# Seven tokens per row, early weight casts, and reciprocals over the GpSimd queue in a fused attention and maxout kernel

## The chip, the cores and the metric

One core of one Trainium2 chip. The time is device microseconds of one execution, as the median over several runs. In the profiles, PE is the matmul engine, PEld its weight loads, DVE the vector engine, ACT the activation engine, POOL GpSimd, and SP the engine that only issues DMAs (SPq is its instruction queue). A run is called slow if it took over 1.5% more than the fastest run of the same kernel; comparisons use the other ("fast") runs.

## The reference

```python
# q, k, v: 8 batches x 12 heads x 448 tokens x 64, float32
scores = cap * tanh(q @ k.T / sqrt(64) / cap)        # cap = 30
attn   = exp(scores - max);  attn /= attn.sum(-1)
x      = (attn @ v)  as (8*448 tokens) x 768
g      = maximum(x @ w1, x @ w2)                     # 768 -> 1024
out    = g @ w_out                                   # 1024 -> 768, float32
```

The kernel computes the last part as relu(x @ (w1 - w2)) @ w_out + x @ (w2 @ w_out); `wd` is the difference, `wm` the product.

## The kernel before

Work goes pair by pair of heads: 48 pairs (numbered 0 to 47), six to a batch. Three pairs share one load of q, k and v (a group), and three share one set of reciprocals of the softmax sums. While a pair's scores go through ACT, PE is filled with matmuls of the batch before. A batch has 448 = 3 x 128 + 64 tokens, so the tokens of a batch stand as three full tiles and a half one, and the two halves of two batches share a tile (`t == 3` below). An SBUF partition p holds the tokens 3p, 3p+1, 3p+2 of the first 384.

Parts (cuts marked):

```python
def invert(g, n0=0, n1=G):            # reciprocals of one group's sums
    nc.vector.reciprocal(t[:m, :], sums[g, n0][:m, :])
    nc.sync.dma_start(out=d[:m, :], in_=t[:m, :])           # "write": SBUF -> DRAM, rec_d
    for h in range(2):                                      # "spread": DRAM -> 64 partitions, rec_b
        nc.sync.dma_start(out=rb[64*h : 64*h+64, ...], in_=flat[h:h+1, :, :].to_broadcast(...))

def moe(b):                            # one batch of the second part
    ...                                # x @ wd -> relu -> g ; then, per tile t of 128 tokens:
        if t == 3:
            ...                        # 64 rows each to two batches
        else:
            rows = out[b0*S : b0*S + NJ*P, :].rearrange("(p j) n -> p j n", j=NJ)
            nc.sync.dma_start(out=rows[:, j, :], in_=osb)   # one DMA of 128 rows of 3072 B

for i in range(N):                     # pair i
    pv_main(i); ...; gather(g)         # sums of a group: SBUF -> SBUF by DMA, after its third pair
    F(8); qk(i+1, 3); ex(i+1, 4, 7)    # F(n): n matmuls of the fill
    for f, a in todo[i]: f(*a)         # this pair's loads and GpSimd casts
    F(6); transposes(i+2); F(6)
    if i >= G and n == 0: invert(g - 1)      # first pair of a group: the group before
    if i >= G and n == 1: normalize(g - 1)   # xT = u * rec_b on GpSimd
    qk(i+2, 0); qk(i+2, 1); ...
```

## Time and profile before

Median 392.37 us of 3 runs (392.2 to 392.74); the profiled execution has a span of 390.3 us at a mean clock of 0.983.

I cut the span in three by the first tanh of pair 11 and of pair 44, as the timeline has them: the start (transfers and ACT bound it, and the weights are prepared), the middle (PE bounds it) and the tail.

| before | us |
|---|---|
| start, to the first tanh of pair 11 | 86.7 |
| middle, pairs 11 to 44 | 225.2 |
| tail, to the end of the span | 78.4 |

The lines of the profile itself stand in the prediction.

### The profile page before, as it was taken

The page shows a single profiled execution, that of the slowest core. Times are in us where ns is not written, and L with a number is a line of the kernel's source. Part 1 is how long each engine was busy: PE and PEld are TensorE (multiplying, and loading weights), DVE is VectorE, ACT ScalarE, POOL GpSimd, SP SyncE. Part 2 cuts the span into 40 slices and gives each one's busy share as a digit, 9 for nine tenths or more (in the row PEclk, how much of TensorE's full clock was granted, in tenths as well). Part 3 has the DMA queues.
Part 4 walks back from the last instruction along what each step waited for, and adds up shares of the span by engine and source line. Part 5 has one row for each costly group of instructions (what it writes and reads, how often), then busy time and mean ns, then how long its engine had stood idle before and what let it go on. Part 6 is the DMA issues. An engine that isn't in the chain of part 4 may idle for free.

```text
span 390.3 us, 5720 instructions
## 1 busy us (share of the span) xinstructions
PE 358.5 (92%) x2128; PEld 171.8 (44%) x2128; DVE 164.3 (42%) x248; ACT 292.4 (75%) x289; POOL 199.6 (51%) x254
## 2 busy tenths in 40 slices
PE   3468896999999999989998999999999999999995
PEld 1123443544444444434443445444444444455563
DVE  5332657774434533253325433352345333633421
ACT  2699995878899799978998899889998899400000
POOL 4272269674638374656657464729482733651000
PEclk9995998999999999999999999999999999999999
DMA  6998899786779768967989597969796751322022
GB/s 142 280 252 180 242 288 274 198 202 165 149 199 252 198 171 199 260 181 192 217 225 223 142 237 210 255 166 225 219 188 179 166 142 65 90 73 100 23 81 81
DMA packets 106596, 71.50 MB, mean 183 GB/s; under 512 B 61384, under 2 KB 99400, under 8 KB 106568
## 3 DMA queue, kind: packets, MB, share of 16 engines
q1 hardware_dynamic: 104616, 67.99, 67.6%
q0 software_dynamic: 1952, 3.15, 4.6%
q8 instruction: 16, 0.26, 0.3%
q14 instruction: 12, 0.10, 0.1%
HBM read 53.48 MB, written 11.18 MB: 166 GB/s over the span
## 4 chain that ended last, share of the span: by engine, by line
PE 54%; DMA 17%; ACT 7%; SPq 6%; POOL 6%; DVE 5%; issue 3%; POOLq 0%; DVEq 0%; ACTq 0%
PE mm L318 15%; PE mm L333 11%; PE mm L330 9%; PE pv L250 8%; DMA rec_d<-rec_s 7%; DMA rec_b<-rec_d 6%; POOL xT L305 6%; PE s L231 5%; ACT expo L238 3%; ACT tanh L232 3%; DMA vm<-in_v_dram 3%; PE pv L259 2%; SPq L112 2%; SPq L101 1%; DMA xT<-in_moe_w_dram 1%
## 5 line engine op out<-in xcount | busy, mean ns | idle before, releaser
L232 ACT ACTIVATE tanh<-s 128x896 bf16<-128x896 f32 x144 | 126.0, 909 | 36.2 <-PE s L231 35.9
L305 POOL TENSOR_TENSOR xT<-u,rec_b 64x448 bf16<-64x448 f32 x95 | 108.2, 1139 | 86.1 <-DMA rec_b<-rec_d 73.8
L238 ACT ACTIVATE expo<-tanh 128x1792 bf16<-128x1792 bf16 x96 | 144.9, 1510 | 3.0
L265 DVE COPY u<-pv 128x896 f32<-128x896 f32 x48 | 52.3, 1091 | 105.3 <-PE pv L259 80.6
L333 PE MATMUL mm<-wo_sb,gT 128*128 128x384 bf16 x448 | 88.8, 327 | 0.0
L318 PE MATMUL mm<-xT,wd_sb 128*128 128x448 bf16 x384 | 80.8, 353 | 3.3 <-POOL xT L305 1.7
L330 PE MATMUL mm<-wm_sb,xT 128*128 128x384 bf16 x336 | 68.0, 327 | 1.8 <-DVE osb L337 1.8
L250 PE MATMUL pv<-expo,vp 128*128 128x448 bf16 x288 | 66.3, 367 | 1.1 <-ACT expo L238 1.1
L333 PEld LDWEIGHTS <-gT 128*128 128x128 bf16 x448 | 41.9, 98 | 36.5 <-issue 10.8
L337 DVE COPY osb<-mm 128x384 f32<-128x384 f32 x56 | 31.0, 555 | 59.9 <-PE mm L333 54.9
L318 PEld LDWEIGHTS <-wd_sb 128*128 128x128 bf16 x384 | 35.4, 98 | 43.9 <-issue 14.5
L231 PE MATMUL s<-qkT 64*128 64x448 bf16 x288 | 46.0, 370 | 7.7 <-DVE qkT L210 5.2
L322 DVE TENSOR_SCALAR gT<-mm 128x448 bf16<-128x448 f32 x64 | 39.9, 623 | 29.6 <-PE mm L318 28.6
L330 PEld LDWEIGHTS <-xT 128*128 128x128 bf16 x336 | 31.7, 98 | 28.6 <-issue 8.7
L250 PEld LDWEIGHTS <-vp 128*128 128x128 bf16 x288 | 28.2, 101 | 29.1 <-issue 7.7
L132 POOL CAST kqf<-qm 128x1152 bf16<-128x1152 f32 x15 | 17.2, 1147 | 33.9 <-DMA qm<-in_q_dram 33.7
L235 ACT ACTIVATE tanh<-s 128x448 bf16<-128x448 f32 x48 | 26.0, 542 | 4.3 <-PE s L234 4.1
L124 POOL CAST vp<-vm 128x576 bf16<-128x576 f32 x30 | 19.9, 665 | 14.2 <-DMA vm<-in_v_dram 9.4
L132 POOL CAST kqf<-km 128x1152 bf16<-128x1152 f32 x15 | 17.2, 1147 | 12.7 <-DMA km<-in_k_dram 11.9
L231 PEld LDWEIGHTS <-qkT 64*128 64x128 bf16 x288 | 10.9, 96 | 22.8 <-issue 15.1
L209 PE MATMUL mm<-ident,kqf 128*128 128x128 bf16 x96 | 9.8, 248 | 11.5 <-DVE kqf L132 7.7
L186 PE MATMUL mm<-wo_sb,w2T 128*128 128x384 bf16 x96 | 18.7, 328 | 0.0
(44 smaller groups left out, 158.9 us busy)
## 6 DMA issues: line engine op xcount, KB each, us to landing
rec_b<-rec_d SPq DMA_DIRECT2D x30, 336.0 KB, 5.0
out_dram<-osb SPq DMA_DIRECT2D x24, 384.0 KB, 3.9
km<-in_k_dram SPq DMA_DIRECT2D x15, 576.0 KB, 7.0
qm<-in_q_dram SPq DMA_DIRECT2D x15, 576.0 KB, 4.5
vm<-in_v_dram SPq DMA_DIRECT2D x15, 576.0 KB, 4.4
xT<-in_moe_w_dram SPq DMA_DIRECT2D x6, 512.0 KB
wo_sb<-in_moe_w_out_dram POOLq DMA_DIRECT2D x4, 384.0 KB, 7.3
gT<-in_moe_w_dram POOLq DMA_DIRECT2D x6, 256.0 KB, 5.8
```

The lines of the kernel that those rows point to most:

```text
L132: eng.tensor_copy(t[:, n0:n1, o : o + NJ, :].rearrange("p n j (h d) -> p n h j d", h=2), m[:, 2 * n0 : 2 * n1, :].rearrange("p (n h) (j d) ...
L231: nc.tensor.matmul(s[:, h, :S], t[r, j * P : (j + 1) * P], qTn[r, :])
L232: nc.scalar.activation(tanh[i][:, 2 * j : 2 * j + 2, :], s[:, :, :S], AF.Tanh, scale=scale / cap)
L238: nc.scalar.activation(expo[i][:, c0:c1, :], tanh[i][:, c0:c1, :], AF.Exp, scale=float(cap))
L250: nc.tensor.matmul(ps[:, h, :S], vp[g % 2][:, n, h, j, :], e[:, 2 * j + h, :], start=(j == 0), stop=False)
L265: nc.vector.tensor_copy(U[g][:, :, n, :], pvt[i][:, :, :S])
L305: eng.tensor_mul(xT[b // 2][r, hp, cs], U[g][r, h, n, :], rec[g, n0][r, n - n0, :])
L318: nc.tensor.matmul(ps[:, :S], wd_sb[:, c, f * P : (f + 1) * P], x[:, c, cs], start=(c == 0), stop=(c == KC - 1))
L322: nc.vector.tensor_relu(g[:, f, cs], ps[:, :S])
L330: nc.tensor.matmul(ps[:, : DM // 2], x[:, c, ts], wm_sb[:, c, hs], start=(c == 0), stop=False)
L333: nc.tensor.matmul(ps[:, : DM // 2], g[:, f, ts], wo_sb[:, f, hs], start=False, stop=(f == FC - 1))
L337: nc.vector.tensor_copy(osb[:, hs], ps[:, : DM // 2])
```

## The change

The intent: in the first two batches (groups 0 to 3, `NT = 4`) a partition row holds seven consecutive tokens, which makes the q and k loads one long row each, with no separate remainder; w_out and w2 are cast by DMA early; the reciprocals stand earlier in the order of work, and their write and spread leave SP for GpSimd's queue. The core of the diff, with cuts:

```diff
+    R7 = S // 64                          # 7
 def load(g, what, ...):
+        if g < NT:                        # q, k: one DMA, rows of 7 tokens
+            nc.sync.dma_start(out=t[...], in_=rows(src, b, h0, h1).rearrange(...))
 ...
 def transposes(i):
-        for j in range(8):                # 8 of 128x128
-            nc.tensor.transpose(ps[:, j*P:(j+1)*P], kqf[g%2][:, n, j, :], ident)
+        for c, to in todo:                # 13 blocks of 64 columns, two 64x64 each, and one 128x128
+            for a in range(2):
+                r = slice(64*a, 64*a+64)
+                nc.tensor.transpose(ps[r, to:to+64], x[r, c:c+D], ident[r, r])
 ...
+    def chain(g):
+        return nc.gpsimd if g > 0 else nc.sync
 def invert(...):
-        nc.sync.dma_start(out=d[:m, :], in_=t[:m, :])
+        chain(g).dma_start(out=d[:m, :], in_=t[:m, :])
+    def spread(...):                      # now a step of its own, on chain(g)
 ...
 def moe(b):
-                rows = out[b0*S : b0*S + NJ*P, :].rearrange("(p j) n -> p j n", j=NJ)
-                nc.sync.dma_start(out=rows[:, j, :], in_=osb)
+                j = t if t < 3 else t - 4
+                o = out[b*S : (b+1)*S, :]
+                if wide: ...              # batches 2 to 7: as before
+                else:
+                    o = o.rearrange("(r j) n -> j r n", j=R7)
+                    nc.sync.dma_start(out=o[2*j : 2*j+2, :, :], in_=osb)
 ...
+    for f in range(0, FC, 2): load_wo(f)  # before the loop, on GpSimd
+    for c in range(3):        load_w2(c)
 ... in the loop over pairs:
+        if i >= G and n == 0: invert(g - 1)         # after F(8) now
         qk(i+1, 3); ex(i+1, 4, 7); for f, a in todo[i]: f(*a)
+        if i >= G and n == 0: spread(g - 1)
+        elif i >= G and n == 1: normalize(g - 1)
         F(6); transposes(i+2); F(6)
-        if i >= G and n == 0: invert(g - 1)
-        if i >= G and n == 1: normalize(g - 1)
```

More of the change, by code (lines that the diff above doesn't have):

```diff
@@ L40 @@
     NJ = 3
+    NT = 4
+    R7 = S // 64
     scale = 1.0 / (D ** 0.5)
@@ L69, with flat @@
     qf = [t[:, :, 4:8, :] for t in kqf]
+    def flat(g):
+        return kqf[g % 2].rearrange("p n j c -> p n (j c)")
     ident = const.tile([P, P], bf16, name="ident")
@@ L89, in half, with rows, raw_of @@
         return slice(0, 64) if b % 2 == 0 else slice(64, P)
+    def rows(t, b, h0, h1):
+        return t[b, h0:h1, :, :].rearrange("h (r j) d -> (h r) (j d)", j=R7)
+    def raw_of(g, what):
+        if (g, what) not in raw:
+            raw[g, what] = stage.tile([P, 2 * L * NJ * D + (2 * L if what == "q" else L) * D], f32, name=what + "r")
+        t = raw[g, what]
+        m = t[:, : 2 * L * NJ * D].rearrange("p (h c) -> p h c", c=NJ * D)
+        l = t[:, 2 * L * NJ * D :].rearrange("p (h d) -> p h d", d=D)
+        return t, m, l
     def load(g, what, n0=0, n1=L):
@@ L94, in load @@
         src = {"k": k, "q": q, "v": v}[what]
-        if (g, what) not in raw:
-            raw[g, what] = (
-                stage.tile([P, 2 * L, NJ * D], f32, name=what + "m"),
-                stage.tile([P, 2 * L if what == "q" else L, D], f32, name=what + "l"),
+        t, m, l = raw_of(g, what)
+        if g < NT and what == "v":
+            x = rows(src, b, h0, h1).rearrange("(h r) c -> r h c", r=64)
+            for a in range(2):
+                nc.sync.dma_start(
+                    out=m[64 * a : 64 * a + 64, 2 * n0 : 2 * n1, :], in_=x[:, :, NJ * D * a : NJ * D * (a + 1)]
+                )
+            for par in range(2):
+                nc.sync.dma_start(
+                    out=l[64 * par : 64 * par + 64, n0:n1, :], in_=x[:, par::2, 2 * NJ * D :]
+                )
+            return
+        if g < NT:
+            nc.sync.dma_start(
+                out=t[:, n0 * S : n1 * S].rearrange("p (n c) -> p n c", c=S),
+                in_=rows(src, b, h0, h1).rearrange("(n p) c -> p n c", p=P),
             )
-        m, l = raw[g, what]
+            return
         nc.sync.dma_start(
@@ L119, in cast @@
         b = g * L // NP
-        m, l = raw[g, what]
+        x, m, l = raw_of(g, what)
         if what == "v":
@@ L128, in cast @@
                 eng.tensor_copy(vl[g % 2][r, n0:n1, r], l[r, n0:n1, :])
+            return
+        if g < NT:
+            x = x[:, n0 * S : n1 * S].rearrange("p (n c) -> p n c", c=S)
+            if what == "q":
+                eng.tensor_copy(flat(g)[:, n0:n1, Q0 : Q0 + S], x)
+                return
+            eng.tensor_copy(flat(g)[:, n0:n1, : NJ * P], x[:, :, : NJ * P])
+            for par in range(2):
+                r = slice(64 * par, 64 * par + 64)
+                eng.tensor_copy(kf[g % 2][r, n0:n1, 3, r], x[r, :, NJ * P :])
             return
@@ L207, in transposes @@
         ps = mm_psum.tile([P, 512], f32, name="mm").bitcast(bf16)
-        for j in range(8):
-            nc.tensor.transpose(ps[:, j * P : (j + 1) * P], kqf[g % 2][:, n, j, :], ident)
-        nc.vector.tensor_copy(qkT_of(g)[:, n, :, :].rearrange("p j c -> p (j c)"), ps)
+        x = flat(g)[:, n, :]
+        todo = [(j * D, (j % 3) * P + (j // 3) * 64) for j in range(6)]
+        odd = i // NP % 2
+        todo += [(Q0 + j * D, Q0 + (64 * j if not odd else 0 if j == 6 else 64 + 64 * j)) for j in range(R7)]
+        for c, to in todo:
+            for a in range(2):
+                r = slice(64 * a, 64 * a + 64)
+                nc.tensor.transpose(ps[r, to : to + 64], x[r, c : c + D], ident[r, r])
+        nc.tensor.transpose(ps[:, NJ * P : Q0], x[:, NJ * P : Q0], ident)
+        nc.vector.tensor_copy(qkT_of(g)[:, n, :, :].rearrange("p j c -> p (j c)")[:, : Q0 + S], ps[:, : Q0 + S])
     def cross(g):
@@ L221, in qk @@
         t = qkT[g][:, n, :, :].rearrange("p j c -> p (j c)")
-        o = Q0 + 64 * (i // NP % 2)
+        o = Q0 + (64 * (i // NP % 2) if g >= NT else 0)
         qTn = t[:, o : o + S]
@@ L278, in gather @@
             )
+    recd = {}
+    def chain(g):
+        return nc.gpsimd if g > 0 else nc.sync
     def invert(g, n0=0, n1=G):
@@ L283, in invert, with spread @@
         nc.vector.reciprocal(t[:m, :], sums[g, n0][:m, :])
-        d = dram.tile([16 * G, 56], f32, name="rec_d")
-        nc.sync.dma_start(out=d[:m, :], in_=t[:m, :])
+        d = recd[g, n0] = dram.tile([16 * G, 56], f32, name="rec_d")
+        chain(g).dma_start(out=d[:m, :], in_=t[:m, :])
+    def spread(g, n0=0, n1=G):
         rb = rec[g, n0] = xpool.tile([P, G, S], f32, name="rec_b")
-        flat = d[:m, :].rearrange("(h n a) c -> h n (a c)", h=2, a=8)
+        lines = recd[g, n0][: 16 * (n1 - n0), :].rearrange("(h n a) c -> h n (a c)", h=2, a=8)
         for h in range(2):
-            nc.sync.dma_start(
+            chain(g).dma_start(
                 out=rb[64 * h : 64 * h + 64, : n1 - n0, :],
-                in_=flat[h : h + 1, :, :].to_broadcast([64, n1 - n0, S]),
+                in_=lines[h : h + 1, :, :].to_broadcast([64, n1 - n0, S]),
             )
@@ L337, in moe @@
                 nc.vector.tensor_copy(osb[:, hs], ps[:, : DM // 2])
+            wide = b * NP >= NT * L
             if t == 3:
                 for n in range(2):
-                    r0 = (b - 1 + n) * S + NJ * P
-                    nc.sync.dma_start(out=out[r0 : r0 + 64, :], in_=osb[64 * n : 64 * n + 64, :])
-            else:
-                b0, j = (b, t) if t < 3 else (b, t - 4)
-                rows = out[b0 * S : b0 * S + NJ * P, :].rearrange("(p j) n -> p j n", j=NJ)
-                nc.sync.dma_start(out=rows[:, j, :], in_=osb)
+                    o = out[(b - 1 + n) * S : (b + n) * S, :]
+                    to = o[NJ * P : S, :] if wide else o.rearrange("(r j) n -> r j n", j=R7)[:, R7 - 1, :]
+                    nc.sync.dma_start(out=to, in_=osb[64 * n : 64 * n + 64, :])
+            else:
+                j = t if t < 3 else t - 4
+                o = out[b * S : (b + 1) * S, :]
+                if wide:
+                    nc.sync.dma_start(out=o[: NJ * P, :].rearrange("(p j) n -> p j n", j=NJ)[:, j, :], in_=osb)
+                else:
+                    o = o.rearrange("(r j) n -> j r n", j=R7)
+                    nc.sync.dma_start(out=o[2 * j : 2 * j + 2, :, :], in_=osb)
     fill_q = []
@@ L358 @@
     NL = N // L
-    NT = 4
     todo = [[] for _ in range(N)]
@@ L365 @@
     for g in range(2, NL):
-        e = 0 if g < NT else 2
-        at(3 * g - 6 - e, load, g, "k")
-        at(3 * g - 5 - e, load, g, "q")
-        at(3 * g - 4, load, g, "v")
-        at(3 * g - (5 if e else 4), cast, nc.gpsimd, g, "k")
-        at(3 * g - (5 if e else 3), cast, nc.gpsimd, g, "q")
-        at(3 * g - 2, cast, nc.gpsimd, g, "v")
-        if g >= NT:
-            at(3 * g - 4, cross, g)
-    at(1, cast, nc.gpsimd, 1, "v")
-    at(0, load_wo, 6)
-    for c in range(KC):
-        at(1 + c, load_w2, c)
+        e = 0 if g > 2 else 1
+        if g < NT:
+            at(3 * g - 7 + e, load, g, "k")
+            at(3 * g - 6, load, g, "q")
+            at(3 * g - 5, load, g, "v")
+            at(3 * g - 5, cast, nc.gpsimd, g, "k")
+            at(3 * g - 4, cast, nc.gpsimd, g, "q")
+        else:
+            at(3 * g - 9, load, g, "k")
+            at(3 * g - 8, load, g, "q")
+            at(3 * g - 5, cast, nc.gpsimd, g, "k")
+            at(3 * g - 5, cast, nc.gpsimd, g, "q")
+            at(3 * g - 4, cross, g)
+            at(3 * g - 7, load, g, "v")
+        todo[3 * g - 3].insert(0, (cast, (nc.gpsimd, g, "v")))
+        if g == 2:
+            at(0, load_w1, 0)
+            at(0, load_w1, 1)
+    for c in range(2, KC):
         at(2 + c, load_w1, c)
+    for c in range(3, KC):
+        at(c - 3, load_w2, c)
     MS = 3
     fill_const(nc.vector, 0)
-    fill_const(nc.gpsimd, 1)
-    load_wo(0)
-    for n0, n1 in ((0, 1), (1, L)):
-        for what in "kqv":
-            load(0, what, n0, n1)
-    for what in "kqv":
-        load(1, what)
-    for what in "kq":
-        cast(nc.vector, 0, what, 0, 1)
+    load(0, "k", 0, 1)
+    load(0, "q", 0, 1)
+    load(0, "k", 1, L)
+    load(0, "q", 1, L)
+    load(0, "v", 0, 1)
+    load(1, "k")
+    load(0, "v", 1, L)
+    load(1, "q")
+    load(1, "v")
+    cast(nc.vector, 0, "k", 0, 1)
+    cast(nc.gpsimd, 0, "q", 0, 1)
+    fill_const(nc.gpsimd, 1)
     transposes(0)
-    cast(nc.vector, 0, "v", 0, 1)
-    for what in "kqv":
-        cast(nc.vector, 0, what, 1, L)
+    cast(nc.vector, 0, "k", 1, L)
+    cast(nc.vector, 0, "q", 1, L)
     qk(0, 0)
@@ L398 @@
     ex(0, 0, 4)
+    transposes(1)
     qk(0, 2)
@@ L401 @@
     ex(0, 4, 7)
+    cast(nc.vector, 0, "v")
     cast(nc.gpsimd, 1, "k")
-    load_wo(2)
     cast(nc.gpsimd, 1, "q")
-    load_wo(4)
-    transposes(1)
+    for f in range(0, FC, 2):
+        load_wo(f)
+    for c in range(3):
+        load_w2(c)
+    cast(nc.gpsimd, 1, "v")
     qk(1, 0)
@@ L435 @@
         F(4 if late else 8)
+        if i == N - 1:
+            invert(g, 0, G - 1)
+        elif i >= G and n == 0:
+            invert(g - 1)
         if i + 1 < N:
@@ L440 @@
             f(*a)
+        if i == N - 1:
+            spread(g, 0, G - 1)
+        elif i >= G and n == 0:
+            spread(g - 1)
+        elif i >= G and n == 1:
+            normalize(g - 1)
         F(6)
@@ L444 @@
         F(6)
-        if i == N - 1:
-            invert(g, 0, G - 1)
-        elif i >= G and n == 0:
-            invert(g - 1)
-        if i >= G and n == 1:
-            normalize(g - 1)
         if i + 2 < N:
@@ L458 @@
     invert(N // G - 1, G - 1, G)
+    spread(N // G - 1, G - 1, G)
     normalize(N // G - 1, 0, G - 1)
```

## The prediction

> **What bounds the kernel now.** I read the busy digits and clock per slice first, then the windows by stage, then the timeline around every place where PE or ACT stood still, then the waits of GpSimd and of the SP queue.
>
> ```profile
> PE   3468896999999999989998999999999999999995
> ACT  2699995878899799978998899889998899400000
> PEclk9995998999999999999999999999999999999999
> DMA  6998899786779768967989597969796751322022
> ```
>
> A slice is 9.76 us. From slice 8 (78 us) PE is always at 9, ACT at 7 to 9. Before that neither is full and DMA is: a start-up fed by transfers, then a long stage on PE, then (ACT at 0 from slice 35) a tail of matmuls alone.
>
> ```profile
> 20.00:40.00 20.00, 15.84 (x90) 6.69 (x86) 7.16 (x9) 19.65 (x21) 9.74 (x17) 0.74 0.99 210
> 60.00:80.00 20.00, 16.27 (x119) 8.52 (x119) 14.94 (x19) 13.47 (x14) 16.13 (x20) 0.91 0.82 215
> 120.00:140.00 20.00, 20.00 (x114) 8.88 (x113) 9.25 (x14) 17.37 (x19) 12.74 (x17) 1.00 0.81 201
> ```
>
> Columns: PE, weight loads, DVE, ACT, GpSimd, clock, DMA share, GB/s. From 20 to 40 us ACT is the bound (19.65 of 20) and DMA is at 0.99; from 60 to 80 us ACT loses 6.5 us; from 120 us PE has no gap.
>
> A busy PE need not be a streaming PE, so I took start-to-start times of successive matmul records. From 90 to 312 us they are 189 ns (448 columns) and 163 ns (384), the rates of the undisturbed tail, with only three stalls, at 166.6, 205.2 and 286.9 us, of 1.45, 1.67 and 0.75 us: 3.3 us above pitch. All else there is work the change leaves alone. From the first tanh of each pair in the timeline, a pair takes 6.81 us over pairs 10 to 44 (79.26 to 311.86 us); ACT alone would need 6.2 (24.5 us for pairs 1 to 5).
>
> The time to win stands at four places. First the start and one stall:
>
> ```profile
> 12.86 1.32 ACT L238 ACTIVATE expo<-tanh 128x1344 bf16<-128x1344 bf16 x1
> 17.14 1.73 ACT L232 ACTIVATE tanh<-s 128x896 bf16<-128x896 f32 x2 [2.96 <-PE s L231]
> ...
> 52.95 0.59 SPq L165 DMA_DIRECT2D xT<-in_moe_w_dram  x1
> 58.73 2.10 DVE L168 TENSOR_TENSOR wd_sb<-xT,gT 128x1024 bf16<-128x1024 f32 x1 [2.97 <-DMA xT<-in_moe_w_dram]
> 60.76 1.08 DVE L265 COPY u<-pv 128x896 f32<-128x896 f32 x1
> 62.35 0.61 PE L209 MATMUL mm<-ident,kqf 128*128 128x128 bf16 x8 [3.13 <-DVE wm_sb L191]
> 64.91 1.73 ACT L232 ACTIVATE tanh<-s 128x896 bf16<-128x896 f32 x2 [4.25 <-PE s L231]
> ```
>
> Pair 1 starts 2.96 us late, because its k and q come in five small loads queued behind v. At 58.7 us the third block of w1, issued only at 52.95, holds DVE; the copies behind it hold PE (3.13) and ACT (4.25). Third, the stalls at 166.6 and 205.2: the next batch's xT is not normalized, as in the second line below. Fourth, the last normalization on DVE waits and blocks copies that free PSUM:
>
> ```profile
> 205.72 1.14 POOL xT L305
> 206.90 0.73 PE mm L318 x3
> ...
> 350.82 0.62 DVE L305 TENSOR_TENSOR xT<-u,rec_b 64x448 bf16<-64x448 f32 x1 [4.46 <-DMA rec_b<-rec_d]
> 352.08 1.14 PE L330 MATMUL mm<-wm_sb,xT 128*128 128x384 bf16 x6 [1.77 <-DVE osb L337]
> ```
>
> The reciprocals' path shows where xT's lateness is born:
>
> ```profile
> SPq L289 <- DMA rec_d<-rec_s: 56.3, 17, 5.4
> POOL xT L305 <- DMA rec_b<-rec_d: 73.8, 31, 8.3
> ```
>
> SP stands 56.3 us in 17 waits for the little write to DRAM, and all loads behind stand with it.
>
> **What the Trainium skill says.** "DMA: Bandwidth & Descriptors", section "Issuing engines are not separate DMA queues": DMAs of any engine share the same 16 DMA engines. So moving a cast load earlier or to another queue adds no bandwidth; the trace agrees, DMA at 0.99 with two queues in use. Same page, "Queues, rings and completion order": each DMA engine takes the queue rows in turn, packet by packet. So a small write on the GpSimd queue need not stand behind all that SP has queued; in this trace, with SP's backlog, that write took up to 5.8 us in the chain. "TensorE: Matmul & The Clock Gate", "Weight-path perf modes": fast weight load is on at 128 weights, and "LDWEIGHTS" there gives columns / 1.2 GHz otherwise. The trace shows a 128-column load at 98 ns and 128-column transposes 56 ns apart, so loads hide; no line of before has a 64-column load.
>
> **The change part by part.**
>
> 1. Start. k and q of pair 0 become one load each, then pairs 1 and 2, v later. q now lands after two issues (issued 1.3 to 1.8 us) instead of after three more; before, it was issued at 2.52 and landed at 5.38, 2.9 us later, so I expect about 4.4 us, less a little GpSimd cast. First tanh about 7.3 instead of 8.13. Transposes of pair 1 now need only k and q, landed by about 6.5; cast about 8.3, transposed about 9.5. Then ACT runs pair 0 without a break: 7.3 + 6.1 = 13.4 instead of 17.14. Gain 3.7 us, kept through pairs 1 to 5 where ACT is the bound: pair 5 at 38.0 instead of 41.64.
>
> 2. Fewer packets. k and q of a group of three pairs go from 1536 packets of 768 B and 768 of 256 B to 768 of 1792 B. By the packet records (mean 42 and 19 ns, 1792 B at a median of 77.5) that is 1536 x 42 + 768 x 19 = 79 us over 16 engines, 4.9 us, to 768 x 77.5 = 60 us, 3.7 us: 1.2 us of DMA time a group, under 5 us for four. The bytes are the same, and w_out and w2 (3.15 MB each in fp32) are only moved forward.
>
> 3. w1. Blocks 0 and 1 are issued two to three pairs earlier, and SP no longer waits for reciprocals after the first group. From the first tanh of pair 7 (54.61 us) to that of pair 8 (64.91) it took 10.3 us, in the unstalled turns around it 6.6 to 6.9 (with one cold stretch after it): the stall is worth 3.9 us. But DMA stays near its limit up to 55 us. Adding the packet times of all that is queued ahead of block 2 (initial loads 12.2, k, q, v of group 2 and two w1 blocks 8.9, w_out and w2 17.8, the rest about 14) gives 53 us of DMA time from 2 us on, and the block is wanted at about 52. I charge a new wait of 1.2 us.
>
> 4. Transposes. Eight of 128x128 become 27, 26 of them 64x64. Now about 8 x 56 = 0.45 us a pair. Two estimates for 64: 29 ns apiece (half the columns), 0.8 us in all; or bound by a 64-column weight load without the fast mode, 53 ns by the skill's formula, 1.4 us. I take +0.7 us a pair. Pairs 2 to 5 are bound by ACT and hide most of it; in the six turns of the loop (4 to 9) that also carry the w2 and w_out products PE is already the bound (6.35 to 7.4 us), so 6 x 0.7 = 4.2 us lost. From pair 12 nothing changes. DVE copies 960 columns instead of 1024, 0.04 us.
>
> Sum at pair 11: 3.7 + 3.9 - 1.2 - 4.2 = 2.2 us, 84.5 instead of 86.66.
>
> 5. Reciprocals. The reciprocal stands two to three us earlier in DVE's order; its write goes out on GpSimd at once, the v cast (2 x 665 + 2 x 346 = 2.0 us) covers the landing, then two spreads. From the issue rows (548 ns for 128 rows, 768 for 256) I estimate 0.4 to 0.5 us for each of the three issues, 1.4 us a group. GpSimd then has 6 x 1.14 + 3.6 + 2.0 + 1.4 = 14 us of work in 20.4 us. From the start of a group's first pair: reciprocal +3, written +6, spread issued +7, landed +11, multiplied +11 to +18; PE wants it at about +22. So the three stalls should go: 3.3 us, of which I count 2.7.
>
> 6. Tail. The last pair's path keeps its length; SP's queueing (rec_d issued 1.2 us after its reciprocal ended at 343.41) goes, GpSimd's first-come order may put some back. I count 0.6 of the 1.9 us.
>
> Total 2.2 + 2.7 + 0.6 = 5.5 us: 392.4 - 5.5 = 386.9.
>
> **The rivals.** (a) Transposes at half cost, and DMA early enough: these six turns lose 2 us instead of 4.2 and no wait for w1: 3.4 us more, 383.5, faster by over 2%. For it: 128-column transposes at 56 ns run at column rate already, and pairs of K = 64 matmuls start 3 ns apart. Against: column-tiled weight loads are unknown here. (b) DMA becomes the early bound: w_out and w2 ahead of k, q and w1 share the engines, and the stall at 58 us moves rather than goes. For it: 0.99 from 20 to 60 us, unchanged bytes. Then only start and reciprocals pay: 3.7 + 3.3 - 4.2, about 389.5. (c) GpSimd's in-order queue: a cast that waits for a load now also holds the reciprocals, and xT comes later than before. For it: GpSimd waited 33.7 us on q loads. Against: q is now loaded one pair earlier, and 14 of 20.4 us leaves room. Then near 390 to 392.
>
> **Range and chances.** Spread: transposes 1.8 us, DMA 1.5, stalls 1, tail 1; together about 2.8, so 8 in 10 lie in 381.8 to 390.8. The 2% line is 384.5, 0.85 of a spread away: with rival (a) I give faster 0.25, same 0.74, slower 0.01.
>
> **What would show it.** Pair 1's tanh near 13.4 us; no wait of 3 us on DVE at w1; first tanh of pair 11 near 84.5; start-to-start of the 64x64 transposes between 29 and 53 ns; no matmul wait for xT after 90 us; pair time 6.7 to 6.8 us thereafter; SP's wait for rec_d nearly gone. Wrong if PE's waits in turns 4 to 9 grow at w2 or w1, if xT waits appear under GpSimd's casts, or if transposes cost 1.5 us a pair or more.

## The result, and the profile after

| | before | changed |
|---|---|---|
| median, same chip | 392.56 us, 4 runs (392.2 to 397.61) | 420.67 us, 4 runs (418.93 to 424.37) |
| profiled span, mean clock | 390.3 us, 0.983 | 417.2 us, 0.949 |
| start | 86.7 | 88.5 |
| middle | 225.2 | 244.3 |
| tail | 78.4 | 84.3 |

The changed kernel is slower: ratio 1.0697, 95% interval 1.0579 to 1.0814. A ratio here and below is the mean time of one kernel's fast runs over that of the other's fast runs of the same rounds, so it is not quite the ratio of the medians.

Of the 26.9 us by which the span grew, 19.1 lie in the middle, where I had predicted a gain of 2.7, and 5.9 in the tail, where I had predicted 0.6 of gain.

The busy digits of the changed kernel, 40 slices of 10.4 us, and under them the clock:

```profile
PE   4674898989994999979994999999999999969996
ACT  4897697878993799957992699989998999200000
PEclk9987799999998899998996899999999999996999
```

Before, PE was at 9, twice at 8, from slice 7 on until the last slice. Now it falls to 4 in slice 12 (125 us), to 7 in slice 17 and to 4 in slice 21 (counted from 0), and ACT falls with it, to 3, 5 and 2. Neither has more to do; both wait, and the clock drops to 8 and 6 behind the gaps. The windows, in the columns of the prediction (PE, weight loads, DVE, ACT, GpSimd, clock, DMA share, GB/s):

```profile
20.00:40.00 20.00, 12.88 (x133) 5.69 (x133) 5.09 (x6) 17.88 (x19) 11.67 (x20) 0.84 1.12 264
...
120.00:140.00 20.00, 14.61 (x69) 5.81 (x68) 4.86 (x8) 11.62 (x12) 8.78 (x12) 0.83 0.77 122
```

From 120 to 140 us PE had been at 20.00 of 20; now it is at 14.61, and the DMA engines move 122 GB/s instead of 201. (The DMA share hardly falls, 0.77 after 0.81, and here it misleads: 344 packet records of 256 B that begin between 126 and 127 us last 304 ns in the mean, though 18 in the median, so some are very long; a microsecond before, the mean was 20 ns. A long record counts as busy whether or not bytes move. The GB/s are the safer number.) The DMA view of the kernel before, digits for 100 to 140 us in slices of 1 us:

```profile
DMA  4799899949960198999956999996998009989930
```

and of the changed kernel in the same stretch:

```profile
DMA  0049998796998999611411111391111159959768
GB/s 0 10 97 213 219 214 107 245 343 145 306 312 213 356 292 254 171 68 59 131 49 55 46 45 55 88 140 52 52 52 52 48 121 290 292 124 362 193 71 260
```

A digit is the mean busy share of 16 engines in tenths. From 120 to 125 and from 127 to 132 us it stands at 1 and the rate at 45 to 55 GB/s: two engines' worth of sixteen (2/16 = 0.125). The packet records say whose packets those are: they have 3072 B, one row of the output. The packets' summed time over the time from the first to the last gives the number in flight:

| output write of 128 rows | packets in flight | us from first to last packet |
|---|---|---|
| before, the six of the first two batches | 11.8, 12.0, 12.5, 5.1, 10.1, 9.1 | 1.4, 1.5, 1.3, 3.5, 2.0, 1.9 |
| changed, the six of the first two batches | 1.6, 1.9, 1.7, 2.0, 2.0, 2.0 | 11.2, 8.2, 10.9, 8.1, 7.6, 8.0 |
| changed, the first three of later batches (from 211 us) | 12.0, 6.9, 10.9 | 1.8, 2.9, 2.0 |

In the mean a write of the first two batches took 1.9 us before and 9.0 now.

The timeline of the changed kernel shows what that costs. Rows are start, duration, engine and line, and in brackets the idle time before and what ended it:

```profile
111.09 7.07 SPq L136 DMA_DIRECT2D qr<-in_q_dram  x1
120.55 3.85 SPq L324 DMA_DIRECT2D sums<-u  x2
124.52 9.04 SPq L263 DMA_TRANSPOSE qkT<-kqf  x1
133.21 0.49 DVE L337 RECIPROCAL rec_s<-sums 48x56 f32<-48x56 f32 x1 [5.29 <-DMA sums<-u]
134.24 0.91 PE L374 MATMUL mm<-xT,wd_sb 128*128 128x448 bf16 x2 [4.96 <-DVE gT L378]
135.74 1.73 ACT L281 ACTIVATE tanh<-s 128x896 bf16<-128x896 f32 x2 [6.56 <-PE s L280]
```

Read it downwards. A small load of 96 KB takes SP 7.07 us only to issue (the kernel before issued such loads in 0.6), and one transpose takes 9.04, where the twelve of the kernel before took 3.7 to 4.8. The gather of the sums, 5 KB, is issued by 124.4 us and DVE waits for it until 133.2, when the second slow write (124.2 to 132.4 us) has ended. Behind the reciprocal in DVE's order stand the copies that free PSUM, so PE stands 4.96 us and ACT 6.56. All three wait for 5 KB. In the kernel before, the same reciprocal found its sums there:

```profile
127.47 0.48 DVE L283 RECIPROCAL rec_s<-sums 48x56 f32<-48x56 f32 x1
```

The other two gaps of the changed kernel wait for other things behind the slow writes: near 187 us PE waits for a transposed k and q, whose DMA took SP 11.40 us to issue, and from 218 us three times for xT (2.87, 2.03 and 1.85 us), whose reciprocal had waited until 204 us for its sums, issued right behind the write of 193 to 201 us (with the writes split, in e1 below, there is one step of 1.69 us instead):

```profile
172.09 11.40 SPq L263 DMA_TRANSPOSE qkT<-kqf  x1
187.40 0.93 PE L280 MATMUL s<-qkT 64*128 64x448 bf16 x4 [2.46 <-DMA qkT<-kqf]
220.86 0.35 PE L374 MATMUL mm<-xT,wd_sb 128*128 128x448 bf16 x1 [2.87 <-POOL xT L361]
```

In the whole middle PE is idle for 14.6 us instead of 2.8. The rest of the 19.1 us, some 7, is the clock behind the gaps: 0.958 in the mean of the middle, where before it was 1.00.

### The profile page after: what moved, and what is told of

Same layout as the page of the kernel before. It is cut to its first block, busy times and chain, and to the rows that moved or that the text cites. A ratio compares the mean times of both kernels' runs of the same rounds, so it can differ in the third digit from the quotient of the medians.

```text
span 417.2 us, 6115 instructions
## 1 busy us (share of the span) xinstructions
PE 369.5 (89%) x2356; PEld 175.0 (42%) x2356; DVE 160.2 (38%) x241; ACT 292.9 (70%) x289; POOL 224.6 (54%) x300
## 4 chain that ended last, share of the span: by engine, by line
PE 58%; DMA 22%; POOL 9%; SPq 4%; issue 3%; ACT 2%; DVE 2%; DVEq 0%; POOLq 0%
PE mm L389 15%; PE mm L374 14%; PE mm L386 11%; PE pv L299 9%; DMA rec_b<-rec_d 7%; POOL xT L361 7%; DMA rec_d<-rec_s 5%; PE s L280 5%; DMA sums<-u 5%; DMA vr<-in_v_dram 4%; PE pv L308 2%; PE s L283 1%; ACT expo L287 1%; SPq L263 1%; SPq L324 1%
## 5 line engine op out<-in xcount | busy, mean ns | idle before, releaser
L374 PE MATMUL mm<-xT,wd_sb 128*128 128x448 bf16 x384 | 86.2, 369 | 12.6 <-POOL xT L361 7.2
L389 PE MATMUL mm<-wo_sb,gT 128*128 128x384 bf16 x448 | 90.1, 330 | 0.0
L386 PE MATMUL mm<-wm_sb,xT 128*128 128x384 bf16 x336 | 69.6, 332 | 4.7 <-DVE osb L393 4.7
L374 PEld LDWEIGHTS <-wd_sb 128*128 128x128 bf16 x384 | 36.4, 100 | 56.9 <-issue 29.4
L284 ACT ACTIVATE tanh<-s 128x448 bf16<-128x448 f32 x48 | 26.0, 542 | 14.9 <-PE s L283 14.7
L345 POOL DMA_DIRECT2D rec_b<-rec_d x32 | 16.8, 531 | 35.5 <-DMA rec_d<-rec_s 35.5
L339 POOL DMA_DIRECT2D rec_d<-rec_s x16 | 8.8, 548 | 48.8 <-DVE rec_s L337 41.0
L154 POOL CAST vp<-vr 128x576 bf16<-128x576 f32 x30 | 20.0, 667 | 4.7 <-DMA vr<-in_v_dram 4.2
L308 PE MATMUL pv<-expo,vl 64*128 64x448 bf16 x96 | 18.0, 371 | 0.0
```

The costliest lines, as they stand in the source:

```text
L308: nc.tensor.matmul(ps[:, h, :S], vl[g % 2][r, n, :], expo[i][r, 6, :], start=False, stop=True)
L374: nc.tensor.matmul(ps[:, :S], wd_sb[:, c, f * P : (f + 1) * P], x[:, c, cs], start=(c == 0), stop=(c == KC - 1))
L386: nc.tensor.matmul(ps[:, : DM // 2], x[:, c, ts], wm_sb[:, c, hs], start=(c == 0), stop=False)
L389: nc.tensor.matmul(ps[:, : DM // 2], g[:, f, ts], wo_sb[:, f, hs], start=False, stop=(f == FC - 1))
```

## The experiments

Twelve kernels, in three sets of four, each set on one chip with seven runs of the kernel before beside it (medians 392.62, 393.82 and 394.11 us). Every output passed the comparison with the reference. The theories at the outset: W, the form of the output write; R, the reciprocal's earlier place in DVE's order; G, GpSimd's in-order queue; D, the early casts.

| stage times of the profiled runs, us | start | middle | tail | median us | ratio to before (95%) |
|---|---|---|---|---|---|
| changed | 88.5 | 244.3 | 84.3 | 420.67 | 1.0697 |
| e1 write split | 89.8 | 224.8 | 83.8 | 400.85 | 1.0214 (1.0159 to 1.0269) |
| b1 before, write 2 x 64 | 85.5 | 254.7 | 78.5 | 421.5 | 1.0731 (1.0692 to 1.0770) |
| b2 before, write 4 x 32 | 85.1 | 238.7 | 80.7 | 406.76 | 1.0337 (1.0285 to 1.0389) |
| e2 reciprocals on SP | 87.2 | 248.0 | 77.9 | 414.19 | 1.0544 (1.0497 to 1.0590) |
| e3 reciprocals late | 90.0 | 246.2 | 82.9 | 428.35 | none, one fast run |
| f1 split, on SP | 86.4 | 221.4 | 77.9 | 388.57 | 0.9881 (0.9807 to 0.9955) |
| h1 split, last group on SP | 87.3 | 225.6 | 78.2 | 393.71 | 1.0019 (0.9949 to 1.0089) |
| f3 split, on SP, late | 92.1 | 225.0 | 78.8 | 399.05 | 1.0156 (1.0073 to 1.0239) |
| f2 split, casts late | 89.9 | 225.5 | 82.5 | 401.57 | 1.0209 (1.0131 to 1.0288) |
| f4 split, on SP, casts late | 90.8 | 221.4 | 78.2 | 389.77 | 0.9910 (0.9835 to 0.9984) |
| g1 f1, first w2 block first | 88.7 | 221.4 | 77.8 | 389.91 | 0.9906 (0.9861 to 0.9952) |
| g2 f1, first group late | 92.8 | 222.2 | 77.9 | 394.15 | 1.0015 (0.9967 to 1.0063) |

One caution for the first column: programs that are alike up to pair 2 reached it anywhere between 19.1 and 21.7 us. A difference of 2 us in the start is no evidence by itself. A row of stages is one run, the profiled one, and not the median: f1's is its fastest (387.41 us), f4's its slowest (392.21 us).

### The output write: e1, b1, b2

e1 takes the changed kernel and writes each tile in two DMAs of 64 rows.

```diff
-                    nc.sync.dma_start(out=o[2*j : 2*j+2, :, :], in_=osb)
+                    for a in range(2):
+                        nc.sync.dma_start(out=o[2*j+a, :, :], in_=osb[64*a : 64*a+64, :])
```

> The changed kernel with one edit: each output write of the first two batches, one DMA of 2x64 rows, becomes two DMAs of 64 rows. Theory W (the 2x64-row write runs on two of the sixteen DMA engines, some 8 us each, and holds everything queued behind it: sums, transposes, loads): the six writes take 2 to 3 us each, the stalls of PE at 129, 184 and 217 to 226 us shrink to under 2 us in sum, the time falls by 14 to 19 us to 400 to 406; what is left is 2 us early and 6 us of tail. Theory R (the reciprocal, moved forward in DVE's order and sent over the GpSimd queue, blocks DVE and GpSimd): nothing of that goes, 415 to 422.

Measured: 400.85 us, 19.8 below the changed kernel's median; the middle fell from 244.3 to 224.8, with PE idle for 2.5 us of it at a clock of 1.00. The six writes took 1.9 to 3.6 us with 5.6 to 13.6 packets in flight. The reciprocal at the place shown above no longer waits, in e1's timeline:

```profile
129.08 0.48 DVE L337 RECIPROCAL rec_s<-sums 48x56 f32<-48x56 f32 x1
```

The reciprocal's early place and GpSimd's queue are still in e1, so neither made the middle slow by itself. Its rows lie as far apart in DRAM as in the changed kernel, so the stride of seven rows didn't either.

b1 is the other half of the proof: the kernel before, with the write form alone, for the first two batches. The rows of a batch then land in the wrong order. It passed the comparison all the same: the rows of a batch are averages over 448 values with nearly equal weights and differ little (a standard deviation over rows of 4.7e-5 against an rms of 4.6e-3, by the reference). That says something about this check, too: it doesn't see a permutation of rows.

```diff
+                if b0 < 2:
+                    o = out[b0*S : (b0+1)*S, :].rearrange("(r j) n -> j r n", j=7)
+                    nc.sync.dma_start(out=o[2*j : 2*j+2, :, :], in_=osb)
+                    continue
```

> The kernel before with the output writes of the first two batches put into the changed kernel's form (rows of out permuted in these batches, so wrong on purpose). Theory W: the six writes take about 8 us each at two engines, the SP queue and the sums come late, 8 to 20 us slower, 400 to 412. Theory R: no change, 391 to 394.

Measured: 421.5 us, 29 above the kernel before, and more than the 8 to 20 that I expected. One DMA's shape makes the kernel before as slow as the whole change did. That the two sums are alike is chance: in b1's middle PE is idle for 26.4 us, in the changed kernel's for 14.6. Why the same writes cost 10 us less there, no run parts; e2 below, with its reciprocals on SP as in b1, is idle for 18.0. Its six writes have 1.9 to 2.0 packets in flight and take 7.6 to 8.9 us; start and tail are as before. The DMA digits of b1, 100 to 140 us:

```profile
DMA  7999994981111111100898993157923971199979
```

b2 gives a smaller dose, 4 x 32 rows in one DMA (rows permuted again):

```diff
+                    o = out[b0*S : (b0+1)*S, :].rearrange("(r j) n -> j r n", j=14)
+                    nc.sync.dma_start(out=o[4*j : 4*j+4, :, :], in_=osb)
```

> Dose for theory W: the kernel before with the output writes of the first two batches as one DMA of 4x32 rows instead of 2x64 (rows permuted, wrong on purpose; bytes and row size as before). If the outermost count sets how many DMA engines a write gets, the six writes run at about 4 packets in flight and take about 4 us each, half of the 8 us at 2x64, and the kernel loses clearly less than the 29 us of 2x64: 396 to 410. If the seven-row stride itself is slow, they stay at 8 us and about 420.

Measured: 406.76 us, 13 above before. In flight 3.3 to 3.7, and 4.5 to 5.6 us per write (two others ran into one another, 12.4 us for both). The tail is 2.3 us longer too, at a clock of 0.84 behind its wait at 362 us, where the kernel before kept 1.00. The digits of b2 show 2 where b1's show 1:

```profile
DMA  6999995993222100897998358996998794232101
```

So the number of packets in flight follows the outermost count of the DMA's target where that is 2 or 4, far below the 5 to 14 that a count of 128 has, and the time follows it. Nothing else differs between b1, b2 and the kernel before but six such writes and the small ones of the left-over rows. The Trainium skill states the rule: "DMA: Bandwidth & Descriptors", section "Why a DMA increments its semaphore by 16 and not by 1", says that a DMA is spread over the largest number of engines, up to 16, that divides the slowest dimension of both sides, so a leading dimension of 2 keeps it to two engines. The 2.0 packets in flight agree. (The records don't name the engine, so that it is always the same two is not shown here.) The undisturbed writes agree: with 12 in flight instead of 2, one expects a factor of 6; 8.0 us against 1.4 is 5.7. With other transfers under way the kernel before has 5 to 10 in flight, and the factor in the mean is 4.7 (9.0 us against 1.9).

### Where the reciprocals are issued: e2, h1, f1

e2 is the changed kernel with the write left at 2 x 64 and all reciprocal DMAs on SP.

```diff
-        return nc.gpsimd if g > 0 else nc.sync
+        return nc.sync
```

> The changed kernel with the reciprocals' DMAs back on the SP queue, all else as changed. Theory W: the slow writes stand ahead of them on the same queue, so the middle stalls stay or grow; only the tail may win up to 6 us: 413 to 425. Theory R: the loss was GpSimd's queue, 398 to 405.

Measured: 414.19 us. The middle stays slow (248.0); the tail falls from 84.3 to 77.9. Two losses, then, with separate causes. The tail of the changed kernel, in its timeline:

```profile
363.97 0.48 DVE L337 RECIPROCAL rec_s<-sums 16x56 f32<-16x56 f32 x1
...
366.57 1.04 POOL L345 DMA_DIRECT2D rec_b<-rec_d  x2 [1.62 <-DMA rec_d<-rec_s]
367.60 0.50 POOL L339 DMA_DIRECT2D rec_d<-rec_s  x1
...
371.44 1.04 POOL L345 DMA_DIRECT2D rec_b<-rec_d  x2 [3.34 <-DMA rec_d<-rec_s]
...
374.79 0.62 DVE L361 TENSOR_TENSOR xT<-u,rec_b 64x448 bf16<-64x448 f32 x1 [7.40 <-DMA rec_b<-rec_d]
376.06 2.08 PE L386 MATMUL mm<-wm_sb,xT 128*128 128x384 bf16 x6 [4.71 <-DVE osb L393]
```

The last pair's reciprocal ends at 364.45. Its write is not issued until 367.60, because ahead of it in GpSimd's queue stands the spread of the two pairs before, which itself waits for its own write. Then the landing (3.34 us of wait), the spread, and DVE can multiply at 374.79: 10.3 us after the reciprocal; before, it was 7.4 (343.41 to 350.82). PE waits 4.71 us, and its clock is 0.50 afterwards: the next 14 matmuls take 4.43 us (376.06 to 380.49) and the 14 after them 2.89, where they take 2.27 at full clock, in f1. That is 2.8 us on top of the longer wait (4.71 where f1, below, has 0.96): 6.5 us by this sum, 6.4 in e2.

f1 does both, the split write and SP. Its tail:

```profile
339.39 0.31 SPq L339 DMA_DIRECT2D rec_d<-rec_s  x1
...
345.94 0.64 DVE L361 TENSOR_TENSOR xT<-u,rec_b 64x448 bf16<-64x448 f32 x1 [3.63 <-DMA rec_b<-rec_d]
...
347.22 1.14 PE L386 MATMUL mm<-wm_sb,xT 128*128 128x384 bf16 x6 [0.96 <-DVE osb L393]
```

The write goes out 0.02 us after its reciprocal ended (338.89 + 0.48), and the multiplication comes 6.6 us after it.

> Split writes, and all reciprocals' DMAs back on the SP queue, still early in the order. The split alone took 400.85 us and lost 5.5 us in the tail and about 3 us before pair 11. Theory G (the tail's loss is GpSimd's queue: the last write and spread wait there in turn, and the normalization on DVE waits for them): the tail from pair 44's first tanh to the end falls from 83.9 to about 78 us, 394 to 396.5. Rival (the tail's loss is the earlier place of the reciprocal on DVE): the tail stays at 83 to 84, 399 to 402.

Measured: 388.57 us (387.41 to 389.18), ratio 0.9881: **the lowest median of all, below both kernels**, though by 1.2%, not by 2 (g1 and f4, below, are within the scatter of it). It beat its expectation by 5 us. The tail gave what it should, 5.9 against e1. What I had not expected is the middle, 221.4 against 224.8. Start-to-start times of matmuls show why: e1 still has three stalls for xT (0.74, 1.69 and 1.13 us long steps at 126.8, 207.6 and 289.3 us), as the kernel before had three, the last two at the same places; f1 has none. One of them, in e1:

```profile
190.18 0.56 POOL L339 DMA_DIRECT2D rec_d<-rec_s  x1 [3.41 <-PE s L283]
...
193.68 1.05 POOL L345 DMA_DIRECT2D rec_b<-rec_d  x2 [0.93 <-DMA rec_d<-rec_s]
...
202.11 7.12 POOL L361 TENSOR_TENSOR xT<-u,rec_b 64x448 bf16<-64x448 f32 x6 [3.71 <-DMA rec_b<-rec_d]
```

From the write to the first multiplication it takes 11.9 us, of which 8.4 are the spread. On SP, for the same group in f1, it is 8.5 and 5.4 (186.22, 189.31, 194.70). Of e1's and f1's difference in the start, 3.4 us, 2.0 is there at pair 2, before any reciprocal has gone over GpSimd, so I don't count it to the queue.

h1 parts the tail from the middle: e1 with the last group alone on SP.

```diff
-        return nc.gpsimd if g > 0 else nc.sync
+        return nc.gpsimd if 0 < g < N // G - 1 else nc.sync
```

> Split writes; only the last group's reciprocal goes back to SP, the other fourteen stay on GpSimd. If the tail's loss is the last group's queueing on GpSimd, the tail from pair 44 falls from 83.8 to about 78 us and the time to 394 to 396.5, between the 400.85 of the split alone and the 388.57 with all on SP; pairs 11 to 44 stay at about 225 us.

Measured: 393.71 us, 0.3 below what I expected; tail 78.2 and middle 225.6, as expected. The last group on GpSimd cost 5.6 us, and leaving the others there costs the 4.2 us of the middle that f1 has and h1 lacks.

### The reciprocal's place in the order: e3, f3, g2

e3 is the changed kernel with reciprocal, spread and normalization back behind the fills, still on GpSimd.

```diff
-        (invert after F(8); spread and normalize after the loads)
+        (all three after the second F(6), as in the kernel before)
```

> The changed kernel with reciprocal and spread moved back behind the fills, where they stood before, still on the GpSimd queue. Theory W: sums still come late behind the slow writes, DVE is blocked less at 129 us, 412 to 421. Theory R: DVE no longer waits for sums ahead of PE's copies, 398 to 406.

Measured: median 428.35, but three of four runs are slow; the one fast run, the profiled one, took 420.92 and has a middle of 246.2. I can give no ratio. It is enough for this much: with the reciprocal back in its old place the middle stays as slow as in the changed kernel, so R is not the cause, and e1 says the same.

f3 adds the late place to f1.

> Split writes, reciprocals on SP and moved back behind the fills. If the early place in DVE's order is what makes DVE wait for the sums at 35 to 41 us (5.7 us there), pair 5 comes 2 to 3 us sooner than with early reciprocals on SP and the time is 1 to 3 us lower than that run's; if DMA is the bound anyway, w1 is then late instead and the two are within 1 us. 392 to 397.

Measured: 399.05 us, above what I expected, and 10.5 above f1. SP's waits say where. In f3:

```profile
SPq L345 <- DMA rec_d<-rec_s: 48.2, 17, 5.0
```

and in f1:

```profile
SPq L345 <- DMA rec_d<-rec_s: 18.5, 15, 2.7
```

(sum of the waits in us, how many, the longest). With write and spread back to back, SP stands between them, and every load stands behind SP. In f1 the loads of that turn lie between the two, and the write lands under their issue. The start suffers most (92.1 against 86.4): the third block of w1 comes late, DVE waits 7.2 us for it and PE 6.7. The early place is the good part of the change, and the GpSimd queue is not what made it pay.

g2 asks how much of that is the first group: f1 with group 0's reciprocal alone in the late place.

> Split writes, reciprocals on SP, only the first group's reciprocal and spread moved back behind the fills. If its early place makes DVE wait for the sums at 35 to 41 us and that costs time in the end, 386 to 388; if SP then waits for that write in one piece and w1 comes late (as with all reciprocals late, 399), pair 7 to 8 takes over 10 us and the time is 392 to 399.

Measured: 394.15 us. The start is 92.8, so that one group carries it: w1's third block is issued at 55.81 us instead of 52.66, and DVE waits 6.22 instead of 2.23, in g2's timeline:

```profile
64.15 1.85 DVE L209 TENSOR_TENSOR wd_sb<-xT,gT 128x1024 bf16<-128x1024 f32 x1 [6.22 <-DMA xT<-in_moe_w_dram]
```

### The early casts: f2, f4, g1

In the changed kernel DMA is at its limit from 20 to 40 us (a share of 1.12 in the windows above, 0.99 before), and the start has a new wait, in its timeline:

```profile
37.86 1.03 PE L216 MATMUL mm<-ident,gT 128*128 128x128 bf16 x8 [3.23 <-DMA gT<-in_moe_w_dram]
...
41.27 0.49 DVE L337 RECIPROCAL rec_s<-sums 48x56 f32<-48x56 f32 x1 [5.70 <-DMA sums<-u]
...
43.58 1.73 ACT L281 ACTIVATE tanh<-s 128x896 bf16<-128x896 f32 x2 [2.38 <-PE s L280]
```

w2's first block comes late, then the sums, and ACT, which bounds this stretch, stands. f2 puts the casts of w_out and w2 back to the places of the kernel before, in e1; f4 does so in f1. (Not to the same times: the first of w_out goes out at 7.5 and 7.8 us instead of 4.2, with a cast of q ahead of it, and the second at 14.9 and 14.5 instead of 18.8.)

```diff
+    load_wo(0) after GpSimd's cast of pair 0's q; load_wo(2), load_wo(4) after the next group's casts of k and q; load_wo(6) at pair 0
+    load_w2(c) at pair 1 + c
-    (all before the loop, or one a pair from pair 0)
```

> Split writes, and the casts by DMA of w_out and w2 issued where the kernel before issued them; reciprocals on GpSimd. Theory D (w_out and w2, cast early, share the DMA engines with v and the sums and hold DVE and PE at 34 to 44 us): first tanh of pair 5 falls from 44.7 to about 40, pair 11 from 89.8 to 86 or less, 396 to 399. Rival (DMA is the bound whatever the order; w2 then comes even later): pair 11 stays at 88 or more, 399 to 403.

> Split writes, reciprocals on SP, casts by DMA at their old times: of the change, the seven-token rows, the new load order and the early reciprocal are left. Theories G and D together: tail 78 us, pair 11 at 85 or less: 389 to 392, at or under the kernel before. If D is wrong: 394 to 397.

Measured: a ratio of 1.0209 for f2, against 1.0214 for e1, and 389.77 us for f4, against 388.57 for f1; no gain in either. Pair 4 to 5 becomes undisturbed (6.1 us in both, where e1 has 10.8 and f1 8.7), but then pair 7 to 8 takes 10.4 us in f2 and 14.1 in f4, waiting for w1 as in the kernel before. My expectation for f4, pair 11 by 85 us, was missed by 6. The wait moves with the order and does not go.

g1 tries the gentlest reordering, f1 with w2's first block cast ahead of w_out.

```diff
+    load_w2(0)
     for f in range(0, FC, 2): load_wo(f)
-    for c in range(3): load_w2(c)
+    for c in range(1, 3): load_w2(c)
```

> Split writes, reciprocals on SP, and the first block of w2 cast ahead of w_out. PE waited 2.4 to 3.3 us at 34 us for that block. If the order is the matter, pair 5 comes 2 us sooner (38.5) and the time falls to 386 to 388; if DMA is the bound early, the wait moves to w_out or w1 and the time stays at 388 to 389.5.

Measured: 389.91 us. The wait for w2 is gone (its transposes start at 34.6 us without one), and in its place DVE waits 4.50 us for the sums and PE 5.67 at 41.8. Three orders, three different waits, and medians within 1.3 us (the start of the profiled runs: 86.4, 90.8 and 88.7). That speaks for the transfers as the bound of the start in any of these orders; no run takes transfers away to show it.

## Why the prediction was wrong

I said 386.9 us, 381.8 to 390.8, and gave slower a chance of 0.01; it was 420.67. The step that failed is a sentence in the reading of the kernel before, "All else there is work the change leaves alone", and its repetition under the transposes, "From pair 12 nothing changes". The prediction's six parts follow the intent of the change; the diff has a hunk for the output write, which got no part. It needed one: six DMAs went from 1.9 us to 9.0 in the mean and held what stood behind them, worth 19.5 us in the middle (changed against e1) or 29 us on the kernel before (b1). None of the three rivals had it either. I had looked up what the skill says of DMA queues, and not how a DMA is spread over engines, on the same page.

Point by point, by its own steps:

1. Start. Right for pair 1 (first tanh at 12.9 us, predicted 13.4, before 17.1). But "kept through pairs 1 to 5" was wrong: v of pair 0 now comes later, and pair 2 starts at 21.0 where before it was 23.4, so 4.2 us had become 2.4 (DVE waits 3.92 us for that v, PE 2.86 for DVE). At pair 5 it is 43.6, later than the 41.6 of before.
2. Fewer packets. No run isolates it, but the packet records show the term mis-sized: it set means (42 and 19 ns) against a median (77.5). In the changed kernel's first 60 us the packets of 1792 B took 78 ns in the median and 95 in the mean, so a group's k and q come to 4.6 us instead of 3.7, against 4.9 before: 0.4 us gained, not 1.2.
3. w1. The 2.97 us wait on DVE shrank to 0.87 (at 60.80 us), and pair 7 to 8 takes 7.6 us instead of 10.3, as predicted in size (3.9 less 1.2). But the stall came back at pair 4 to 5, 10.4 us instead of 6.1. That is rival (b), "the stall at 58 us moves rather than goes", and f2, f4 and g1 agree with it.
4. Transposes. The term was mis-sized. From the first start to the last end the 27 take 0.76 us at full clock, the 8 of before 0.61: 0.15 us a pair instead of 0.7, so 0.9 us over the six turns instead of 4.2. The records show why: the two halves of a column block start 3 to 4 ns apart, and a block follows the one before after 32 ns when the clock is full. My 29 ns was nearly the right step, but two transposes share it: 13 steps, 0.4 us. The skill says so in "TensorE: Matmul & The Clock Gate", "Part 3: Packing small matmuls — row/col tiling": tiles in different row groups overlap, with starts about 4 ns apart. The trace agrees, with 3 to 4. Rival (a) was right in this half, and most of the 4.2 us were never lost.
5. Reciprocals. Half right. The three stalls can go, and are worth about what I said: 3.4 us in the middle from e1 to f1, 3.3 predicted at most. But not over GpSimd's queue, where the spread took 8.4 us where I had allowed 4. It takes the early place, with loads between write and spread (f1 against f3), and SP (f1 against e1). Why the spread is slower from GpSimd's queue, no run parts.
6. Tail. Wrong in sign: 5.9 us lost instead of 0.6 gained. I wrote "GpSimd's first-come order may put some back"; it put back ten times what I had counted. This is rival (c), which I had thought of for the casts in the middle, and not for the two chains of the tail which stand in one queue (e2, h1).

With the write split and the reciprocals on SP, f1 has 86.4, 221.4 and 77.9 us in the three stages where the prediction's steps come to 84.5, 222.5 (225.2 less 2.7) and 77.8 (78.4 less 0.6); a pair of its middle takes 6.71 us, as predicted (6.7 to 6.8), and its 388.57 us lies in the range. That is in part luck. The 84.5 contains 4.2 us for the transposes that cost 0.9; with the right size the other steps of the start promise 81.2, and f1 has 86.4: it starts pair 1 earlier by 3.8 us, pair 5 by 1.0 and pair 7 later by 1.1. So the gains of the start were overstated by about as much as its loss. And step 5 was to work over GpSimd's queue, where it didn't. What decided was the step that I hadn't worked out.

Three readings in the prediction are off, without weight in its sum: PE isn't always at 9 from slice 8 (8 in slices 20 and 24, 5 in the last); pairs 10 to 44 take 6.84 us each ((311.86 - 79.26) / 34), not 6.81; 24.5 us over four pairs are 6.1, not 6.2. And at 166.6 us the trace has PE waiting for a DVE copy (osb), and not for xT itself; that copy stood behind one of u, which had waited 4.22 us for xT.

What stays open: how SP's issue comes to last 7 to 11 us behind a slow write. A full queue would explain it, but no run shows that.

## What to carry to other kernels

Go through a diff hunk by hunk, and ask of every DMA whose shape changes what its outermost count is; one with a count of 2 took nearly five times as long here in the mean, and what it cost was not its own time but that of what stood behind it: sums of 5 KB, a transpose. Split such a write, or put the large dimension outermost. Before moving a chain of small DMAs to another in-order queue, look for two such chains that meet in it; leaving work between a write and its dependent read on the old queue gained more than the move.

## What the Trainium skill lacked or had wrong

- "DMA: Bandwidth & Descriptors", "Why a DMA increments its semaphore by 16 and not by 1": the rule holds (1.6 to 2.0 packets in flight for a leading 2, 3.3 to 3.7 for 4, 5 to 14 for 128). What it lacks is the cost to others: a 5 KB gather issued by 124.4 us was waited for until 133.2, and SP's issue of a 96 KB load lasted 7.07 us. Six writes of 393 KB, at 7.6 to 8.9 us each, cost the kernel before 29 us (b1).
- "DMA: Bandwidth & Descriptors", "Anatomy of one DMA": it gives a fixed cost of about 2.0 us for a DMA from GpSimd. In the tail, from the issue of the small write to the issue of the spread that waits for it took 2.2 us (364.40 to 366.57) when nothing was ahead, and 3.8 (367.60 to 371.44) right after another spread was issued. No figure for that second case is given.
- "TensorE: Matmul & The Clock Gate", "LDWEIGHTS": columns / 1.2 GHz makes 53 ns for a load of 64 columns. 26 such loads in alternating row groups took 0.49 us in an undisturbed row: a record lasts 110 ns, and they start 15 ns apart in the mean. So the formula gives neither the length of a record nor the rate there. The page's Part 3 says that loads overlap with matmuls in flight in other row groups, and gives no rate for such loads.
